# A gated linear attention followed by a SoLU layer: two kinds of small matmul cut into pieces of 32 weight columns

## The chip, the core and the metric

The kernel runs on one core of a Trainium2 chip, in one launch. The metric is device time in microseconds, the median of several executions. One further execution was profiled; every duration, wait and order in time below is from that one. TensorE appears in the profile as two rows, PE for matmuls and PEld for weight loads; VectorE is DVE, ScalarE is ACT, GpSimd is POOL, SyncE is SP.

## What is computed

Four batch entries, eight heads, 768 steps, head dimension 48. A complex state is decayed and updated at each step; the output is read from its real part. Its result, 3072 tokens of 384, goes through a two-layer network of width 1024 with a softmax gate and a layer norm between:

```python
mag = np.sqrt(a_re * a_re + a_im * a_im)
scale = np.minimum(mag, 0.999) / (mag + 1e-06)
for t in range(S):
    new_re = ar * S_re - ai * S_im
    new_im = ar * S_im + ai * S_re
    S_re, S_im = (new_re + einsum('bhd,bhe->bhde', k[t], v[t]), new_im)
    y[:, :, t] = einsum('bhd,bhde->bhe', q[t], S_re)
x = y.transpose(0, 2, 1, 3).reshape(B * S, H * D)
h = x @ w_in
solu = h * softmax(h)
ln = (solu - mean) / np.sqrt(var + 1e-06) * g_ln
out = ln @ w_out
```

All data is fp32.

## The kernel before

The recurrence is computed in chunks of 128 steps, six chunks in time (`ti`) for each of four batch entries (`b`), so 24 chunks in all. The complex decay is turned into cumulated magnitudes and phases, and q and k are multiplied by them with cosine and sine side by side (`f_q2`, `f_k2`: 96 columns a head). Within a chunk the steps are then plain matmuls. The main loop is unrolled: each turn weaves together the preparation of the next `ti` (`prep_steps`), the attention of chunk n (`chunk_steps`), the network of chunk n-1 (`ffn_steps`), and the turning of q and k of chunk n+1 (`turn_steps`). There is a second, general program (`general`) in the file; a flag computed at run time decides whether it is needed, and it is not run here.

The steps that the change and the prediction touch:

- `score` (L768): for each head, scores of a chunk, keys by queries, 128 x 128 over a contraction of 96, into `f_score`. VectorE masks them into `f_att` (L770), half a chunk (four heads) at a time.
- `values` (L774 to L786): for each head, `f_att` (128 x 128) is the stationary operand (`lhsT`, "weights") and the head's 48 columns of v stream through (L779). From the second `ti` on a second matmul adds the contribution of the state: the queries `f_qT` (96 x 128) are the weights, and 48 columns of `f_state` stream (L782). Both write the same 128 partitions x 48 columns of one PSUM bank, the tile `f_y`. VectorE copies the tile to `f_xn` (L785).
- `carry` (L788 to L800): for each head, `f_k2` (128 x 96) is the weights and the 48 columns of v stream, into 96 partitions of the tile `f_d`, which has the same single PSUM buffer as `f_y` (pool `f_ps_y`). VectorE adds it to the state and GpSimd multiplies it by the chunk's total decay.
- `ffn_steps`: `f_xt` is the transposed x (L814), `f_h` = x by `w_in` (two halves of three products of 512 columns, L824), the maximum (L832), the exponential (L833), the product `f_z` (L836), its transposes `f_zt` (L845), the statistics, and `f_o` = z by `w_out` (eight products of 384 columns, L870).
- `f_turned` (L747) are the transposes of q and k; `f_L` (L659) and `f_phase` (L700, L703) are the cumulated sums of `prep_steps`; `f_tot` (L684) is a transpose of 32 rows, five times in all; `f_count` (L889) is a one-column matmul at the end of the attention, once.

The order on TensorE, VectorE, GpSimd and SyncE is set by the framework's scheduler, which takes the instructions in the woven order and places them by its own costs and by what is ready; only ScalarE's order is that of the program. Each queue is then in order. SyncE issues all DMAs. An fp32 product becomes two weight loads and two matmuls in the trace (384 matmuls at L779 for 24 x 8 products); the transposes become one of each.

Of the kernel before, what the change touches and what calls it, by code (L numbers as in the profile page):

```python
# [17 lines left out]
P = 128  # L18
# [493 lines left out]
def whole(ctx, tc, flag, q, k, v, a_re, a_im, moe_w_in, moe_w_out, moe_g_ln, out):  # L512
# [8 lines left out]
    nc = tc.nc  # L521
    B, H, S, D = q.shape
    D2 = 2 * D
# [28 lines left out]
    state = [const.tile([D2, DM], FP, name=f"f_state{b}") for b in range(B)]  # L552

    seen = const.tile([P, 3, NC], FP, name="f_seen")
    T = {}

    def heads(t):
        return t.rearrange("p (h d) -> p h d", d=D)
# [198 lines left out]
    def chunk_steps(ti, b):  # L757
        st = {}

        def score(half):  # L760
            def f():
                if half == 0:
                    st["att"] = two.tile([P, H, P], FP, tag="att", name="f_att")
                QT, KT = T["qT", ti, b], T["kT", ti, b]
                ps = ps_s.tile([P, 4, P], FP, tag="s", name="f_score")
                for i in range(4):
                    x = half * 4 + i
                    nc.tensor.matmul(out=ps[:, i], lhsT=KT[:, x * P:(x + 1) * P], rhs=QT[:, x * P:(x + 1) * P],  # L768
                                     start=True, stop=True)
                nc.vector.tensor_tensor(out=st["att"][:, half * 4:half * 4 + 4], in0=ps,  # L770
                                        in1=tri.unsqueeze(1).to_broadcast([P, 4, P]), op=OP.mult)
            return f

        def values():  # L774
            V = T["v", ti][:, b]
            y = ps_y.tile([P, DM], FP, tag="y", padded_shape=[P, 512], name="f_y")
            for x in range(H):
                ys = y[:, x * D:(x + 1) * D]
                nc.tensor.matmul(out=ys, lhsT=st["att"][:, x], rhs=V[:, x * D:(x + 1) * D], start=True,  # L779
                                 stop=(ti == 0))  # L780
                if ti > 0:
                    nc.tensor.matmul(out=ys, lhsT=T["qT", ti, b][:, x * P:(x + 1) * P],  # L782
                                     rhs=state[b][:, x * D:(x + 1) * D], start=False, stop=True)
            xt = xp.tile([P, DM], FP, tag="x", name="f_xn")
            nc.vector.tensor_copy(out=xt, in_=y)  # L785
            T["x", ti, b] = xt  # L786

        def carry():  # L788
            V = T["v", ti][:, b]
            d = ps_y.tile([D2, DM], FP, tag="y", padded_shape=[P, 512], name="f_d")  # L790
            for x in range(H):
                nc.tensor.matmul(out=d[:, x * D:(x + 1) * D],  # L792
                                 lhsT=T["k2", ti, b][:, x].rearrange("p u d -> p (u d)"),
                                 rhs=V[:, x * D:(x + 1) * D], start=True, stop=True)
            tot = T["tot", ti][:, b * H:(b + 1) * H].unsqueeze(2).to_broadcast([D2, H, D])
            if ti > 0:
                nc.vector.tensor_tensor(out=state[b], in0=d, in1=state[b], op=OP.add)  # L797
                nc.gpsimd.tensor_tensor(out=heads(state[b]), in0=heads(state[b]), in1=tot, op=OP.mult)  # L798
            else:
                nc.vector.tensor_tensor(out=heads(state[b]), in0=heads(d), in1=tot, op=OP.mult)  # L800

        steps = [score(0), score(1), values]
        if ti < NC - 1:
            steps.append(carry)
        return steps
# [106 lines left out]
    for n in range(len(chunks) + 1):  # L912
        ti, b = chunks[n] if n < len(chunks) else (NC, 0)
# [76 lines left out]
```

## Time and profile before

| | |
|---|---|
| median of 3 runs | 747.02 us (746.8 to 751.04) |
| the profiled execution | 743.38 us |
| its span, first to last instruction | 741.6 us |
| mean granted TensorE clock over the span | 0.878 |
| PE busy / PEld busy | 588.8 us / 416.1 us, 2887 instructions each |
| VectorE, ScalarE, GpSimd busy | 380.3, 246.4, 171.3 us |
| f_y, value part (L779) | 384 matmuls, mean 285 ns |
| f_y, state part (L782) | 320 matmuls, mean 290 ns |
| f_d (L792) | 320 matmuls, mean 286 ns |

A row of the profile names the line, the engine, the operation, the tile written and the tiles read, the shape and the count, then busy time, the mean of one in ns, and the idle time of the engine just before with what ended it. In a row of the timeline the first number is the start and the second the length of a merged group. Matmuls are pipelined: the mean of one contains the latency of reading its operands, several are in flight, and the distance between starts is less than the duration. In the views by stretches of time each engine has its busy time and its count, then come the granted clock, the share of the DMA engines and the bandwidth.

### The profile page before, as it was taken

The page shows a single profiled execution, that of the slowest core. Times are in us where ns is not written, and L with a number is a line of the kernel's source. Part 1 is how long each engine was busy: PE and PEld are TensorE (multiplying, and loading weights), DVE is VectorE, ACT ScalarE, POOL GpSimd, SP SyncE. Part 2 cuts the span into 40 slices and gives each one's busy share as a digit, 9 for nine tenths or more (in the row PEclk, how much of TensorE's full clock was granted, in tenths as well). Part 3 has the DMA queues.
Part 4 walks back from the last instruction along what each step waited for, and adds up shares of the span by engine and source line. Part 5 has one row for each costly group of instructions (what it writes and reads, how often), then busy time and mean ns, then how long its engine had stood idle before and what let it go on. Part 6 is the DMA issues. An engine that isn't in the chain of part 4 may idle for free. (4 is left out here: it accounts for less than half of the span.)

```text
span 741.6 us, 7378 instructions
## 1 busy us (share of the span) xinstructions
PE 588.8 (79%) x2887; PEld 416.1 (56%) x2887; DVE 380.3 (51%) x590; ACT 246.4 (33%) x325; POOL 171.3 (23%) x133
## 2 busy tenths in 40 slices
PE   0215217768998988998988989898989989999994
PEld 0104204535667665767665766675766757766652
DVE  2489985646526447525537344457354673322331
ACT  2435040214234354236233244334343542222211
POOL 2072565530112050221222021412020420000000
PEclk9955658669996999998989999989989999999997
DMA  9834722040420050520040420223310000000000
GB/s 170 159 74 100 132 64 64 22 82 15 96 54 0 11 97 0 96 54 6 6 96 7 89 54 11 56 42 69 62 20 11 12 0 11 11 11 11 11 11 17
DMA packets 131788, 35.55 MB, mean 48 GB/s; under 512 B 126752, under 2 KB 129824, under 8 KB 131744
## 3 DMA queue, kind: packets, MB, share of 16 engines
q1 hardware_dynamic: 131744, 34.98, 23.9%
q8 instruction: 25, 0.41, 0.2%
q14 instruction: 19, 0.16, 0.1%
HBM read 30.22 MB, written 4.72 MB: 47 GB/s over the span
## 5 line engine op out<-in xcount | busy, mean ns | idle before, releaser
L870 PE MATMUL f_o<-f_w_out,f_zT 128*128 128x384 f32 x384 | 139.8, 512 | 0.0
L824 PE MATMUL f_h<-f_w_in,f_xT 128*128 128x512 f32 x288 | 130.8, 597 | 0.6 <-ACT f_xT L817 0.6
L870 PEld LDWEIGHTS f_o<-f_w_out,f_zT 128*128 128x128 f32 x384 | 74.4, 204 | 44.0 <-issue 7.0
L862 POOL TENSOR_TENSOR f_s<-f_s,f_mv 128x1 f32<-128x1 f32 x24 | 19.7, 822 | 314.5 <-DVE f_s L861 186.0
L824 PEld LDWEIGHTS f_h<-f_w_in,f_xT 128*128 128x128 f32 x288 | 53.2, 190 | 58.8 <-issue 51.7
L779 PE MATMUL f_y<-f_v,f_att 128*128 128x48 f32 x384 | 73.2, 285 | 14.6 <-DVE f_att L770 14.5
L833 ACT ACTIVATE f_z<-f_h,f_nmax 128x1024 f32<-128x1024 f32 x24 | 26.7, 1113 | 148.0 <-DVE f_nmax L832 125.3
L779 PEld LDWEIGHTS f_y<-f_v,f_att 128*128 128x128 f32 x384 | 61.1, 204 | 19.7 <-DVE f_att L770 15.4
L782 PE MATMUL f_y<-f_state,f_qT 96*128 96x48 f32 x320 | 65.9, 290 | 0.0
L832 DVE TENSOR_REDUCE f_nmax<-f_h 128x1 f32<-128x1024 f32 x24 | 29.3, 1223 | 60.0 <-PE f_h L824 60.0
L768 PEld LDWEIGHTS f_score<-f_qT,f_kT 96*128 96x128 f32 x384 | 53.2, 201 | 9.3 <-issue 6.8
L768 PE MATMUL f_score<-f_qT,f_kT 96*128 96x128 f32 x384 | 56.9, 283 | 0.0
L876 DVE TENSOR_SCALAR f_ot<-f_o,f_rs 128x384 f32<-128x384 f32 x24 | 14.8, 616 | 77.4 <-PE f_o L870 38.5
L750 ACT COPY f_kT<-f_turned 96x512 f32<-96x512 f32 x48 | 27.8, 579 | 80.2 <-PE f_turned L747 80.2
L792 PE MATMUL f_d<-f_v,f_k 128*96 128x48 f32 x320 | 40.0, 286 | 16.7 <-DVE f_xn L785 16.7
L782 PEld LDWEIGHTS f_y<-f_state,f_qT 96*128 96x128 f32 x320 | 52.7, 206 | 0.0
L792 PEld LDWEIGHTS f_d<-f_v,f_k 128*96 128x96 f32 x320 | 39.3, 207 | 19.5 <-DVE f_xn L785 17.6
L770 DVE TENSOR_TENSOR f_att<-f_score,f_mats 128x512 f32<-128x512 f32 x48 | 32.9, 685 | 28.5 <-PE f_score L768 28.5
L659 PE MATMUL f_L<-f_lr,f_mats 128*128 128x384 f32 x48 | 21.3, 538 | 32.6 <-DVE f_lr L652 32.6
L846 ACT COPY f_zT<-f_zt 128x512 f32<-128x512 f32 x48 | 26.5, 585 | 59.6 <-PE f_zt L845 59.6
L750 ACT COPY f_qT<-f_turned 96x512 f32<-96x512 f32 x48 | 28.0, 583 | 52.9 <-PE f_turned L747 52.8
L798 POOL TENSOR_TENSOR f_state<-f_state,f_tot 96x384 f32<-96x384 f32 x16 | 19.1, 1192 | 112.3 <-DVE f_state L797 110.7
(93 smaller groups left out, 896.1 us busy)
## 6 DMA issues: line engine op xcount, KB each, us to landing
f_ar<-in_a_re_dram SPq DMA_DIRECT2D x24, 192.0 KB, 4.0
f_ai<-in_a_im_dram SPq DMA_DIRECT2D x24, 192.0 KB, 4.5
f_q<-in_q_dram SPq DMA_DIRECT2D x24, 192.0 KB, 4.5
f_k<-in_k_dram SPq DMA_DIRECT2D x24, 192.0 KB, 4.0
f_v<-in_v_dram SPq DMA_DIRECT2D x24, 192.0 KB, 4.2
out_dram<-f_ot SPq DMA_DIRECT2D x24, 192.0 KB, 2.0
f_raw<-in_moe_w_in_dram SPq DMA_DIRECT2D x6, 512.0 KB, 4.6
f_raw<-in_moe_w_out_dram SPq DMA_DIRECT2D x8, 384.0 KB, 3.1
```

The costliest lines, as they stand in the source:

```text
L659: nc.tensor.matmul(out=ps, lhsT=tri, rhs=lm, start=True, stop=True)
L750: nc.scalar.copy(out=T[nm + "T", ti, b][:, half * 512:half * 512 + 512], in_=ps[0:D2].rearrange("p i t -> p (i t)"))
L768: nc.tensor.matmul(out=ps[:, i], lhsT=KT[:, x * P:(x + 1) * P], rhs=QT[:, x * P:(x + 1) * P], start=True, stop=True)
L770: nc.vector.tensor_tensor(out=st["att"][:, half * 4:half * 4 + 4], in0=ps, in1=tri.unsqueeze(1).to_broadcast([P, 4, P]), op=OP.mult)
L779: nc.tensor.matmul(out=ys, lhsT=st["att"][:, x], rhs=V[:, x * D:(x + 1) * D], start=True, stop=(ti == 0))
L782: nc.tensor.matmul(out=ys, lhsT=T["qT", ti, b][:, x * P:(x + 1) * P], rhs=state[b][:, x * D:(x + 1) * D], start=False, stop=True)
L792: nc.tensor.matmul(out=d[:, x * D:(x + 1) * D], lhsT=T["k2", ti, b][:, x].rearrange("p u d -> p (u d)"), rhs=V[:, x * D:(x + 1) * D], star ...
L824: nc.tensor.matmul(out=st["h"][:, half * 512:(half + 1) * 512], lhsT=st["xT"][:, c * P:(c + 1) * P], rhs=w_in[:, c, half * 512:(half + 1) ...
L832: nc.vector.tensor_reduce(out=nmax, in_=st["h"], op=OP.max, axis=AX.X, negate=True)
L833: nc.scalar.activation(out=st["z"], in_=st["h"], func=AF.Exp, bias=nmax, accum_out=st["se"])
L846: nc.scalar.copy(out=st["zT"][:, half * 512:(half + 1) * 512], in_=ps)
L870: nc.tensor.matmul(out=st["o"], lhsT=st["zT"][:, c * P:(c + 1) * P], rhs=w_out[:, c], start=(c == 0), stop=(c == KF - 1))
```

## The change

The two matmuls of `values` and the one of `carry` are written as loops over groups of 32 weight columns. Each piece takes 32 columns of the weights, streams the same 48 columns through them, and writes the group of 32 PSUM partitions that belongs to those columns. `values` has four groups, `carry` three. The order within a head is: the four value pieces, then the four state pieces. Operands, buffers, results and all other steps are as before.

```diff
--- before.py
+++ after.py
@@ -774,13 +774,15 @@
         def values():
             V = T["v", ti][:, b]
             y = ps_y.tile([P, DM], FP, tag="y", padded_shape=[P, 512], name="f_y")
+
             for x in range(H):
-                ys = y[:, x * D:(x + 1) * D]
-                nc.tensor.matmul(out=ys, lhsT=st["att"][:, x], rhs=V[:, x * D:(x + 1) * D], start=True,
-                                 stop=(ti == 0))
-                if ti > 0:
-                    nc.tensor.matmul(out=ys, lhsT=T["qT", ti, b][:, x * P:(x + 1) * P],
-                                     rhs=state[b][:, x * D:(x + 1) * D], start=False, stop=True)
+                hs = slice(x * D, (x + 1) * D)
+                for g in range(0, P, 32):
+                    nc.tensor.matmul(out=y[g:g + 32, hs], lhsT=st["att"][:, x, g:g + 32], rhs=V[:, hs], start=True,
+                                     stop=(ti == 0))
+                for g in range(0, P if ti > 0 else 0, 32):
+                    nc.tensor.matmul(out=y[g:g + 32, hs], lhsT=T["qT", ti, b][:, x * P + g:x * P + g + 32],
+                                     rhs=state[b][:, hs], start=False, stop=True)
             xt = xp.tile([P, DM], FP, tag="x", name="f_xn")
             nc.vector.tensor_copy(out=xt, in_=y)
             T["x", ti, b] = xt
@@ -789,9 +791,9 @@
             V = T["v", ti][:, b]
             d = ps_y.tile([D2, DM], FP, tag="y", padded_shape=[P, 512], name="f_d")
             for x in range(H):
-                nc.tensor.matmul(out=d[:, x * D:(x + 1) * D],
-                                 lhsT=T["k2", ti, b][:, x].rearrange("p u d -> p (u d)"),
-                                 rhs=V[:, x * D:(x + 1) * D], start=True, stop=True)
+                hs, k2 = slice(x * D, (x + 1) * D), T["k2", ti, b][:, x].rearrange("p u d -> p (u d)")
+                for g in range(0, D2, 32):
+                    nc.tensor.matmul(out=d[g:g + 32, hs], lhsT=k2[:, g:g + 32], rhs=V[:, hs], start=True, stop=True)
             tot = T["tot", ti][:, b * H:(b + 1) * H].unsqueeze(2).to_broadcast([D2, H, D])
             if ti > 0:
                 nc.vector.tensor_tensor(out=state[b], in0=d, in1=state[b], op=OP.add)
```

On TensorE 352 products of f_y become 1408 and 160 of f_d become 480. The framework gives each piece an array shape of 128 rows by 32 columns, where the whole products have 128 by 128. Of the other matmuls of the program that runs only `f_tot` (32 by 128) and `f_count` (128 by 32) have a shape of their own. Between neighbours on TensorE the shape changes 120 times after the change and 12 times before. The scheduler also orders anew; line numbers behind the change have moved (L779 is L781, L782 is L784, L792 is L796, L845 is L847, L870 is L872).

The first place is on TensorE in a later chunk, of the second batch entry, at the end of `values` (the number at the end of a name is a buffer's). Before:

```order
L779 MATMUL f_y<-f_v,f_att 128x48
L782 MATMUL f_y<-f_state_119,f_qT 128x48
L845 MATMUL f_zt<-f_mats,f_z 128x128 x8
L792 MATMUL f_d<-f_v,f_k_900 96x48 x3
L870 MATMUL f_o<-f_w_out,f_zT 128x384 x8
L684 MATMUL f_tot<-f_mats,f_e_1252 96x32
L747 MATMUL f_turned<-f_mats,f_k_918 96x128 x4
L792 MATMUL f_d<-f_v,f_k_900 96x48 x5
```

With the change:

```order
L781 MATMUL f_y<-f_v,f_att 32x48 x4
L784 MATMUL f_y<-f_state_119,f_qT 32x48 x3
L847 MATMUL f_zt<-f_mats,f_z 128x128 x8
L784 MATMUL f_y<-f_state_119,f_qT 32x48
L781 MATMUL f_y<-f_v,f_att 32x48 x4
L784 MATMUL f_y<-f_state_119,f_qT 32x48 x4
L872 MATMUL f_o<-f_w_out,f_zT 128x384 x7
L684 MATMUL f_tot<-f_mats,f_e_1524 96x32
L747 MATMUL f_turned<-f_mats,f_k_1038 96x128 x4
L747 MATMUL f_turned<-f_mats,f_q_1029 96x128 x4
L872 MATMUL f_o<-f_w_out,f_zT 128x384
L796 MATMUL f_d<-f_v,f_k_1020 32x48 x24
```

The eight transposes f_zt now stand inside f_y, with nine of its 64 pieces behind them, and f_d, which stood in two parts around f_o, now stands in one part behind it.

The second place is on TensorE in a chunk of the first `ti`, where there is no state part yet. Before:

```order
L779 MATMUL f_y<-f_v,f_att 128x48 x8
L792 MATMUL f_d<-f_v,f_k_262 96x48 x8
L845 MATMUL f_zt<-f_mats,f_z 128x128 x8
L747 MATMUL f_turned<-f_mats,f_k_888 96x128 x4
L870 MATMUL f_o<-f_w_out,f_zT 128x384 x4
```

With the change:

```order
L781 MATMUL f_y<-f_v,f_att 32x48 x32
L847 MATMUL f_zt<-f_mats,f_z 128x128 x8
L796 MATMUL f_d<-f_v,f_k_262 32x48 x4
L747 MATMUL f_turned<-f_mats,f_k_1008 96x128 x4
L872 MATMUL f_o<-f_w_out,f_zT 128x384 x4
L747 MATMUL f_turned<-f_mats,f_q_995 96x128 x4
L872 MATMUL f_o<-f_w_out,f_zT 128x384 x4
L796 MATMUL f_d<-f_v,f_k_262 32x48 x20
```

Here f_d stood directly behind f_y and now comes behind f_zt, in two parts with transposes and f_o between them.

## The prediction

> **What bounds the kernel now.** I read the page's busy shares and slices first, then the same by stretches of time, then who waits for whom.
>
> ```profile
> PE 588.8 (79%) x2887; PEld 416.1 (56%) x2887; DVE 380.3 (51%) x590; ACT 246.4 (33%) x325; POOL 171.3 (23%) x133
> PE   0215217768998988998988989898989989999994
> PEclk9955658669996999998989999989989999999997
> 320.00:426.00 106.00, 96.40 (x503) 70.25 (x502) 53.26 (x82) 40.61 (x54) 22.82 (x17) 0.94 0.22 45
> 426.00:532.00 106.00, 96.39 (x503) 70.17 (x502) 53.42 (x83) 40.63 (x54) 22.82 (x17) 0.94 0.23 45
> L832 DVE TENSOR_REDUCE f_nmax<-f_h 128x1 f32<-128x1024 f32 x24 | 29.3, 1223 | 60.0 <-PE f_h L824 60.0
> ```
>
> From about 200 us on TensorE is the bound: in each 106 us (four chunks, one for each batch index) PE is busy 96.4, VectorE 53, and VectorE's longest idle time ends with a matmul. The granted clock there is 0.94, so work that is costed at full clock is stretched by about 1/0.93 = 1.075 (0.92 to 0.94 in the five stretches from 215 us on). What a product costs on PE therefore goes almost whole into the time. The next question is what paces the products that are split.
>
> ```profile
> L779 PE MATMUL f_y<-f_v,f_att 128*128 128x48 f32 x384 | 73.2, 285 | 14.6 <-DVE f_att L770 14.5
> L782 PE MATMUL f_y<-f_state,f_qT 96*128 96x48 f32 x320 | 65.9, 290 | 0.0
> L792 PE MATMUL f_d<-f_v,f_k 128*96 128x48 f32 x320 | 40.0, 286 | 16.7 <-DVE f_xn L785 16.7
> 415.97 0.39 PE L782 MATMUL f_y<-f_state,f_qT 96*128 96x48 f32 x2
> ...
> 419.10 0.39 PE L782 MATMUL f_y<-f_state,f_qT 96*128 96x48 f32 x2
> 419.32 1.06 PE L845 MATMUL f_zt<-f_mats,f_z 128*128 128x128 f32 x8
> 421.15 2.75 PE L870 MATMUL f_o<-f_w_out,f_zT 128*128 128x384 f32 x8
> 423.73 0.60 PE L747 MATMUL f_turned<-f_mats,f_q 128*96 128x128 f32 x4
> 426.75 0.97 PE L792 MATMUL f_d<-f_v,f_k 128*96 128x48 f32 x10
> 427.56 0.61 PE L747 MATMUL f_turned<-f_mats,f_k 128*96 128x128 f32 x4
> L779 PEld LDWEIGHTS f_y<-f_v,f_att x384: 186/192/338, 74.0 to 707.3; 128*128 128x128 f32 x192
> L792 PEld LDWEIGHTS f_d<-f_v,f_k x320: 159/165/284, 87.9 to 635.5; 128*96 128x96 f32 x160
> ```
>
> Twenty-four chunks of 8 heads are 192 products at L779, and the trace has 384: an fp32 product runs as two passes, each with its own weight load. Durations of matmuls overlap, so I take distances between starts. From 415.97 to 419.10 lie 14 rows of two passes: 3.13/28 = 112 ns a pass. f_o streams 384 columns in (423.73 - 421.15)/8 = 322 ns, 0.84 ns a column; at that rate a pass over 48 columns needs 40 ns, so f_y is not paced by its matmul. The load of 96 weight columns (median 165 ns) is 27 ns shorter than that of 128 (192), again 0.84 ns a column, and f_d's passes come every (427.56 - 426.75)/10 = 81 ns. Both are paced by weight columns: 128 x 0.84 = 108 and 4 over for f_y, 96 x 0.84 = 81 for f_d. At full clock f_y costs 352 products x 2 x 112 = 78.8 us and f_d 160 x 2 x 81 = 25.9: 104.7 us, a seventh of the span.
>
> **The change, part by part.**
>
> *The passes.* 352 products of f_y become 1408 pieces, 160 of f_d become 480. That is 1888 pieces, 3776 passes for 1024. Weight columns in total are the same, bytes streamed as moving operand are three to four times as many. A pass now has 32 x 0.84 = 27 ns of load and 40 ns of streaming. If different column groups stream at the same time, while loads still come one after another with the 4 ns that f_y's pass has beyond its columns, a pass costs 31 ns. The bounds of this unknown are wide. Below: the two passes of one piece use the same group and cannot share it, so a piece takes at least one 40 ns stream plus 4, with its other pass beside the neighbour's first: 44 ns a piece, 22 a pass. Above: 81 ns, the fastest sustained pass that the trace shows, as if a pass could not be issued faster. I take 31, because loads that stand one behind another are what paces these very rows now. f_y: 8 x 31 - 224 = +24 ns a product, 352 of them, +8.4 us. f_d: 6 x 31 - 162 = +24 ns, 160 of them, +3.8. Together +12.2.
>
> *Going in and out of the narrow form.* All but six matmuls of the path that runs use the array in one shape. One exception is the count of L889, one column wide, and it shows what an excursion costs.
>
> ```profile
> 677.02 0.59 ACT L750 COPY f_qT<-f_turned 96x512 f32<-96x512 f32 x1
> 677.56 0.39 PE L768 MATMUL f_score<-f_qT,f_kT 96*128 96x128 f32 x2
> 677.88 0.09 PEld L889 LDWEIGHTS f_count<-f_good,f_mats 128*1 128x1 f32 x2
> 677.88 0.20 PE L889 MATMUL f_count<-f_good,f_mats 128*1 128x18 f32 x2
> 678.01 0.71 PE L768 MATMUL f_score<-f_qT,f_kT 96*128 96x128 f32 x4
> 678.12 0.17 DVE L892 TENSOR_REDUCE f_total<-f_count 1x1 f32<-1x18 f32 x1 [1.34 <-PE f_count L889]
> 678.56 0.59 PE L824 MATMUL f_h<-f_w_in,f_xT 128*128 128x512 f32 x1
> L889 PE MATMUL f_count<-f_good,f_mats x2: 178/178/178, 677.9 to 677.9; 128*1 128x18 f32 x2
> ```
>
> From 677.56 to 678.56 run six score passes and two of the count. Six at 112 are 0.67 us; two matmuls of 178 ns fill 0.20, so they start about 25 ns apart, 0.05 for both. The other 0.28 us is neither: the count's input was ready (VectorE had been idle 1.34 us) and the buffer's last reader, at 677.02, had ended by 677.61. So 0.28 us is what one trip out of the full shape and back costs. The Trainium skill, TensorEngine Tiling, Key Properties, says that a change of tiling mode drains the engine; the trace agrees with 0.28 us, and without that rule the same row would be called a chance gap and this term nothing. In the changed order 120 neighbours differ in shape where 12 did: 54 more trips, 54 x 0.28 = 15.1 us. Below, nothing, if a long matmul ahead hides the drain; above, this sum. I take the sum, since nothing in that row hid it.
>
> *What is moved.* The scheduler now cuts f_y around f_zt and moves f_d behind f_o. The cut is in the trips. The copy f_xn comes some 0.9 us later there, behind eight transposes, but seven f_o passes cover it before f_d needs the bank. No DMA and no VectorE, ScalarE or GpSimd instruction is added.
>
> *What swallows part.* PE itself waits in places:
>
> ```profile
> PE f_y L779 <- DVE f_att L770: 14.5, 5, 3.6
> PE f_zt L845 <- DVE f_se L860: 12.7, 6, 3.9
> 417.62 1.23 DVE L836 TENSOR_TENSOR f_z<-f_h,f_z 128x1024 f32<-128x1024 f32 x1 [0.67 <-ACT f_z L833]
> ```
>
> Growth ahead of such a wait costs nothing: 8 products x 24 ns x 5 and 16 x 24 ns x 6, about 3 us.
>
> *The sum*, at full clock 12.2 + 15.1 = 27.3, times 1.075 = 29, less 3: +26 us. The profiled execution took 743.38 us (span 741.6), so 769; the runs' median of 747.02 lies 3.6 above it, so I forecast 773 on the runs' scale. Its own range is 757 to 782 (trips free; trips as said and 33 ns a pass).
>
> **The rivals.**
>
> *Groups work fully side by side.* Loads of different groups overlap too, and a piece costs the lower bound of 44 ns: f_y 4 x 44 - 224 = -48 ns, -16.9 us; f_d 3 x 44 - 162 = -30, -4.8. With the trips that is -21.7 + 15.1 = -6.6, times 1.075 -7: 736, on the runs' scale 740; with trips hidden -23 (724). The place is the f_y stretch, and the deciding price is a piece of (104.7 - 15.1)/1888 = 47 ns: under it the change is not slower. For it: the pieces write different partitions. The Trainium skill, TensorEngine Tiling, Key Properties, says that different tiles can load and multiply in parallel; no row here shows it. Against it: part cannot be collected. f_z is done at 418.85 and f_zt starts at 419.32, so f_y may end at most 0.47 us sooner in such a chunk, where 16 products would save 0.77; with half of the twenty later chunks so, 3 us are lost.
>
> *Streams take turns.* Matmuls of different groups do not overlap; each pass costs 40 + 4 = 44 ns. f_y 8 x 44 - 224 = +128, +45.1 us; f_d 6 x 44 - 162 = +102, +16.3. With trips 76.5, times 1.075 82, less up to 4 in waits: +78, 821, on the runs' scale 825. For it: every stream in the trace is one after another. Against: none there uses another group.
>
> *Instructions can't be had fast enough.* The passes bring 5504 more instructions to PE's queue.
>
> ```profile
> 725.90 0.72 PEld L845 LDWEIGHTS f_zt<-f_mats,f_z 128*128 128x128 f32 x4 [4.70 <-issue]
> 725.93 0.88 PE L845 MATMUL f_zt<-f_mats,f_z 128*128 128x128 f32 x3 [3.90 <-DVE f_se L860]
> ```
>
> After a wait, with PE empty, the matmul starts 30 ns behind its load. At 30 ns an instruction, 60 a pass, f_y grows by 256 ns (90.1 us), f_d by 198 (31.7); with trips 137, times 1.075 147: 890, and 894 on the runs' scale. At 81 a pass it would be 979. Against it: the count's two passes start 25 ns apart, though four waiting instructions say little on a stream of 256. The Trainium skill, TensorE: Matmul & The Clock Gate, Part 1, gives about 62 ns a matmul where the sequencer decodes in its own code; by that figure my estimate is 902 on the runs' scale; no row here tells which way it is decoded.
>
> **How the numbers follow.** The forecast has 0.45, side by side 0.22, taking turns 0.20, instructions 0.13. The range 734 to 833 holds the forecast, taking turns, and side by side with its trips; left out are the instructions and part of side by side with trips hidden, under 2 in 10. About 1% is what a measurement of this kernel can tell from no change. Faster by over 1% needs side by side with trips largely hidden, half of its chance: 0.11. Within 1%: its other half and the forecast's low end, 0.11 + 0.06 = 0.17. Slower: 0.72.
>
> **What would show it.** In the profile after: f_y's passes start about 31 ns apart (rows of four pieces, eight passes, every 250 ns), and the first full-width row after a stretch comes some 0.2 us late. Distances of 22 ns would show side by side, 44 turns, 60 or more the supply of instructions. Granted clock in the stretches stays between 0.90 and 0.95. The forecast is wrong if f_y's stretch of 16 products, 3.5 us before, gets shorter, or takes more than 5 us; or if f_y keeps to 4 us and the time still moves by over 5%.

## The result: 4.3% faster

| | before | after |
|---|---|---|
| median | 746.91 us (4 runs) | 716.14 us (4 runs) |
| ratio, 95% interval | | 0.957 (0.951 to 0.963) |
| span of the profiled execution | 741.6 us | 714.8 us |
| PE busy / the rest of the span | 588.8 / 152.8 us | 533.9 / 180.9 us |

The forecast was 773, slower, with a range down to 734. The time lies outside it and on the other side. The page of the changed kernel, first the busy shares, the granted clock by slices, and the groups that answer to those shown of before:

```profile
PE 533.9 (75%) x5639; PEld 344.4 (48%) x5639; DVE 379.4 (53%) x590; ACT 245.7 (34%) x325; POOL 170.6 (24%) x133
PEclk9955658769997989997989997999989999999998
L781 PE MATMUL f_y<-f_v,f_att 128*32 128x48 f32 x1536 | 39.6, 214 | 21.8 <-DVE f_att L770 21.8
L847 PE MATMUL f_zt<-f_mats,f_z 128*128 128x128 f32 x192 | 31.9, 320 | 25.0 <-DVE f_se L862 16.5
L796 PE MATMUL f_d<-f_v,f_k 128*32 128x48 f32 x960 | 24.7, 240 | 21.2 <-DVE f_xn L787 21.2
```

PE's busy time fell by 54.9 us though it has nearly twice the instructions; its idle time rose by 28.1; the difference, 26.8, is what the span lost. Three waits hold most of the rise: for f_att 21.8 us (14.5 before), ahead of f_zt 25.0 (12.7), for f_xn 21.2 (16.7), together 24. (f_se, named ahead of f_zt, is an operation of 0.14 us right behind f_z on VectorE; what f_zt reads is f_z.) So there are two things to explain: why the pieces are so much cheaper than forecast, and where half of that went. The timeline of one chunk of the changed kernel answers both:

```profile
402.05 0.29 PE L781 MATMUL f_y<-f_v,f_att 128*32 128x48 f32 x8
402.16 0.27 PE L784 MATMUL f_y<-f_state,f_qT 96*32 96x48 f32 x8
...
402.69 0.27 PE L784 MATMUL f_y<-f_state,f_qT 96*32 96x48 f32 x8
403.14 0.29 PE L781 MATMUL f_y<-f_v,f_att 128*32 128x48 f32 x8 [0.19 <-DVE f_att L770]
...
403.78 0.27 PE L784 MATMUL f_y<-f_state,f_qT 96*32 96x48 f32 x8
405.13 1.06 PE L847 MATMUL f_zt<-f_mats,f_z 128*128 128x128 f32 x8 [1.09 <-DVE f_z L838]
412.66 0.79 PE L796 MATMUL f_d<-f_v,f_k 128*32 128x48 f32 x40
413.38 0.64 PE L747 MATMUL f_turned<-f_mats,f_k 128*96 128x128 f32 x4
```

From 402.16 to 402.69 six rows of eight passes start, one product each: 88 ns a product, 11 ns a pass, where a product took 224 before. That is two streams of 40 ns plus 4 for eight passes, so all four column groups stream at once, and the loads of their weights (32 columns, 27 ns at 0.84 a column) overlap too: four loads fit into 44 ns. f_d's 40 passes take 0.72 us with the way out of the narrow shape (some 0.14), 14 to 15 a pass at full clock: three groups at once, 86 ns a product for 162. And PE now stands still: at the seam between the halves of `f_att`, and for 1.09 us ahead of f_zt, where before f_z had been ready 0.47 us early.

### The profile page after: what moved, and what is told of

Read it like the earlier page. It is cut to its first block, busy times and chain, and to the rows that moved or that the text cites. A ratio compares the mean times of both kernels' runs of the same rounds, so it can differ in the third digit from the quotient of the medians.

```text
span 714.8 us, 12886 instructions
## 1 busy us (share of the span) xinstructions
PE 533.9 (75%) x5639; PEld 344.4 (48%) x5639; DVE 379.4 (53%) x590; ACT 245.7 (34%) x325; POOL 170.6 (24%) x133
## 5 line engine op out<-in xcount | busy, mean ns | idle before, releaser
L872 PE MATMUL f_o<-f_w_out,f_zT 128*128 128x384 f32 x384 | 143.2, 520 | 0.3 <-ACT f_zT L848 0.3
L872 PEld LDWEIGHTS f_o<-f_w_out,f_zT 128*128 128x128 f32 x384 | 75.3, 207 | 44.2 <-issue 8.0
L781 PE MATMUL f_y<-f_v,f_att 128*32 128x48 f32 x1536 | 39.6, 214 | 21.8 <-DVE f_att L770 21.8
L768 PEld LDWEIGHTS f_score<-f_qT,f_kT 96*128 96x128 f32 x384 | 50.8, 193 | 9.3 <-issue 6.8
L768 PE MATMUL f_score<-f_qT,f_kT 96*128 96x128 f32 x384 | 54.8, 277 | 0.0
L847 PE MATMUL f_zt<-f_mats,f_z 128*128 128x128 f32 x192 | 31.9, 320 | 25.0 <-DVE f_se L862 16.5
L781 PEld LDWEIGHTS f_y<-f_v,f_att 128*32 128x32 f32 x1536 | 32.1, 113 | 30.4 <-DVE f_att L770 24.2
L747 PE MATMUL f_turned<-f_mats,f_k 128*96 128x128 f32 x192 | 37.1, 326 | 13.0 <-DVE f_k L724 8.4
L796 PE MATMUL f_d<-f_v,f_k 128*32 128x48 f32 x960 | 24.7, 240 | 21.2 <-DVE f_xn L787 21.2
L847 PEld LDWEIGHTS f_zt<-f_mats,f_z 128*128 128x128 f32 x192 | 25.4, 164 | 28.7 <-issue 15.8
```

Source lines behind the costliest of these rows:

```text
L747: nc.tensor.transpose(out=ps[0:D2, i], in_=T[nm + "2", ti, b][:, half * 4 + i].rearrange("p u d -> p (u d)"), identity=ident)
L781: nc.tensor.matmul(out=y[g:g + 32, hs], lhsT=st["att"][:, x, g:g + 32], rhs=V[:, hs], start=True, stop=(ti == 0))
L796: nc.tensor.matmul(out=d[g:g + 32, hs], lhsT=k2[:, g:g + 32], rhs=V[:, hs], start=True, stop=True)
L847: nc.tensor.transpose(out=ps[:, i * P:(i + 1) * P], in_=st["z"][:, c * P:(c + 1) * P], identity=ident)
L872: nc.tensor.matmul(out=st["o"], lhsT=st["zT"][:, c * P:(c + 1) * P], rhs=w_out[:, c], start=(c == 0), stop=(c == KF - 1))
```

## The experiments

The theory: column groups have queues and streams of their own, so a product costs two streams; what TensorE saves is partly waited away for VectorE. The rivals: narrow pieces are cheap whatever group they use; the gain comes from the new order of the other instructions; the trips between shapes are free. Ratios are to the kernel before on the same chip, with 95% intervals.

**The same pieces, one group behind the other.**

```diff
-            for x in range(H):
-                hs = slice(x * D, (x + 1) * D)
-                for g in range(0, P, 32):
+            for x0, g in ((x0, g) for x0 in range(0, H, 4) for g in range(0, P, 32)):
+                for x in range(x0, x0 + 4):
+                    hs = slice(x * D, (x + 1) * D)
                     nc.tensor.matmul(out=y[g:g + 32, hs], lhsT=st["att"][:, x, g:g + 32], rhs=V[:, hs], start=True,
                                      stop=(ti == 0))
-                for g in range(0, P if ti > 0 else 0, 32):
-                    nc.tensor.matmul(out=y[g:g + 32, hs], lhsT=T["qT", ti, b][:, x * P + g:x * P + g + 32],
-                                     rhs=state[b][:, hs], start=False, stop=True)
+                    if ti > 0:
+                        nc.tensor.matmul(out=y[g:g + 32, hs], lhsT=T["qT", ti, b][:, x * P + g:x * P + g + 32],
+                                         rhs=state[b][:, hs], start=False, stop=True)
```

> The same pieces as in the change, as many trips between shapes, but ordered so that the pieces of one column group stand behind one another (four heads of one group, then four of the next). Theory A, groups stream side by side and a group can't overlap with itself: a pass costs the 40 ns stream plus 4 again, a product of f_y 8 x 44 = 352 ns for 87 now, 352 products, +93 us at full clock, about +100 by the granted clock, of which up to 20 vanish in waits: 795 to 816 us. Rival B, narrow pieces are quick in themselves, whatever group they use: starts stay 6 to 11 ns apart and the time stays at 716 within 1%. Rival C, the gain came from the new order of the other instructions, which this kernel shares: 716 too, but with starts 44 ns apart.

735.68 us, ratio 0.986 (0.980 to 0.992): 20 us more than the change, not 80. Its timeline:

```profile
401.83 0.27 PE L781 MATMUL f_y<-f_v,f_att 128*32 128x48 f32 x2
401.94 0.25 PE L784 MATMUL f_y<-f_state,f_qT 96*32 96x48 f32 x2
402.03 0.25 PE L781 MATMUL f_y<-f_v,f_att 128*32 128x48 f32 x2
402.12 0.25 PE L784 MATMUL f_y<-f_state,f_qT 96*32 96x48 f32 x2
402.20 0.25 PE L781 MATMUL f_y<-f_v,f_att 128*32 128x48 f32 x2
402.29 0.25 PE L784 MATMUL f_y<-f_state,f_qT 96*32 96x48 f32 x2
402.38 0.28 PE L781 MATMUL f_y<-f_v,f_att 128*32 128x48 f32 x4
402.46 0.28 PE L784 MATMUL f_y<-f_state,f_qT 96*32 96x48 f32 x4
402.58 0.25 PE L781 MATMUL f_y<-f_v,f_att 128*32 128x48 f32 x2
...
402.93 0.28 PE L781 MATMUL f_y<-f_v,f_att 128*32 128x48 f32 x4
```

Within one group two passes start every 87 to 90 ns, 44 a pass: a group can't overlap with itself, and the passes cost four times as much as when the next one uses another group. That ends the rival of cheap narrow pieces. The order of the other instructions is the change's, and the time is 736 and not 716, so that order alone does not bring the gain. But at the seams (rows of four) the last passes of one group run beside the first of the next, so 16 passes take 0.55 us (402.38 to 402.93), not 0.70: a product costs 275 ns, not 352, and f_y 66 us more than in the change. Why only 20 of these come out, the waits and the windows of this kernel tell:

```profile
PE f_d L796 <- DVE f_xn L787: 15.4, 7, 11.2
PE f_y L781 <- DVE f_att L770: 12.4, 5, 2.8
PE f_zt L847 <- DVE f_se L862: 10.4, 6, 3.9
PE f_zt L847 <- DVE f_z L838: 0.9, 1, 0.9
```

```profile
207.00:308.00 101.00, 91.21 (x956) 63.42 (x955) 54.02 (x80) 38.99 (x52) 20.50 (x16) 1.00 0.25 45
308.00:408.00 100.00, 91.60 (x991) 65.00 (x991) 52.97 (x79) 39.05 (x52) 22.70 (x15) 0.97 0.26 48
```

The waits for f_att, f_z (with f_se) and f_xn are 39 us where the change has 68, and the granted clock is 0.97 to 1.00 in these stretches, where the change has:

```profile
207.00:308.00 101.00, 85.93 (x1009) 56.96 (x1008) 53.52 (x82) 40.20 (x54) 21.98 (x16) 0.92 0.26 48
308.00:408.00 100.00, 84.93 (x1004) 56.14 (x1004) 53.40 (x82) 40.27 (x54) 23.00 (x17) 0.91 0.26 49
```

Slower matmuls fill the waits, and the clock comes back. The first is a matter of counting; what moves the clock was not tried. It is no small term. Against the kernel before, this one pays 18 us more for f_y (275 ns for 224) and up to 14 for the trips, and saves 12 at f_d: some 20 us more at full clock, and yet it takes 10 us less. PE's idle time is nearly the same, 148.5 us for 152.8; the mean granted clock over the span is 0.927 for 0.878, worth some 32 us on 581 us of matmuls (an estimate). The change itself has 0.885, so by the same estimate the clock makes no more than some 4 us of its gain.

**Four passes of one group in a row.**

```diff
                 for g in range(0, P, 32):
                     nc.tensor.matmul(out=y[g:g + 32, hs], lhsT=st["att"][:, x, g:g + 32], rhs=V[:, hs], start=True,
                                      stop=(ti == 0))
-                for g in range(0, P if ti > 0 else 0, 32):
-                    nc.tensor.matmul(out=y[g:g + 32, hs], lhsT=T["qT", ti, b][:, x * P + g:x * P + g + 32],
-                                     rhs=state[b][:, hs], start=False, stop=True)
+                    if ti > 0:
+                        nc.tensor.matmul(out=y[g:g + 32, hs], lhsT=T["qT", ti, b][:, x * P + g:x * P + g + 32],
+                                         rhs=state[b][:, hs], start=False, stop=True)
```

> The change with each group's value piece and state piece of a head behind one another: four passes of one group in a row, then the next group. If passes must start in program order, as the forecast had it, they go three serial passes of 44 ns and then one beside the next group's first: a head costs 4 x 132 + 44 = 572 ns for 174, 160 heads, +64 us at full clock, and some 20 in the time as with 16 in a row (736). If each group has a short queue of its own, four passes deep or more by what the seams of the run with 16 in a row show: a head still costs 174 to 200 ns and the time is 716 within 1%.

716.04 us, ratio 0.959 (0.952 to 0.966): the same as the change. The program, in the order that the scheduler leaves on TensorE, alternates value and state, a piece (two passes) at a time; the starts do not:

```profile
403.94 0.31 PE L781 MATMUL f_y<-f_v,f_att 128*32 128x48 f32 x8
404.05 0.29 PE L784 MATMUL f_y<-f_state,f_qT 96*32 96x48 f32 x8
404.14 0.29 PE L781 MATMUL f_y<-f_v,f_att 128*32 128x48 f32 x7
404.23 0.21 PE L784 MATMUL f_y<-f_state,f_qT 96*32 96x48 f32 x1
404.24 0.21 PE L781 MATMUL f_y<-f_v,f_att 128*32 128x48 f32 x1
```

Eight value passes, of all four groups, start ahead of the first state pass, though the program has two, then two of the other, and so on. So passes of different groups start out of program order; four in a row are held back for their group while the others go on, and 16 in a row are too many, where only the seams overlap. The Trainium skill, TensorE: Matmul & The Clock Gate, Part 3 (The mechanism), says that matmuls start and end in program order; these rows show that matmuls of different column groups do not start in it, and the measurement decides. So the sentence ahead of the prediction that each queue is in order does not hold for these matmuls.

**Half of the change, and the other half.** Values in pieces with the state update whole, and the reverse. The first undoes this part of the change, the second the part in `values`:

```diff
-                for g in range(0, D2, 32):
-                    nc.tensor.matmul(out=d[g:g + 32, hs], lhsT=k2[:, g:g + 32], rhs=V[:, hs], start=True, stop=True)
+                nc.tensor.matmul(out=d[:, x * D:(x + 1) * D],
+                                 lhsT=T["k2", ti, b][:, x].rearrange("p u d -> p (u d)"),
+                                 rhs=V[:, x * D:(x + 1) * D], start=True, stop=True)
```

> Only the matmuls of values in pieces, the state update whole. At full clock f_y saves (224 - 87) ns x 352 = 48 us of TensorE's time; 35 more trips between shapes, some 0.16 us each by the trace of the change, take 6. If everything TensorE saves came out: 747 - 45 = 702. If, as in the whole change, about half comes out and the rest turns into waits: 722 to 728. If the state update carries most of the gain: 740 or more.

> Only the state update in pieces, values whole. f_d saves about (162 - 66) ns x 160 = 15 us; 32 more trips of 0.16 us take 5. All out: 736. Half out: 741 to 743. If the parts add, this and the run with values alone together give the change's 31 us; if a wait is shared between them, together they give more than 31.

727.64 us, ratio 0.974 (0.969 to 0.980), and 738.22 us, ratio 0.989 (0.983 to 0.995). The first has its half coming out as expected. For the second the expectation counted too much: with 86 ns a product f_d saves 12 us and not 15, and with the 0.26 us a trip that is measured below 32 trips take 8, which leaves 4 at full clock. The measured 8 us (4 to 12 by the interval) are all of that or more, not half; in its profiled execution PE's busy time is 8.1 us less than before and the span 5.4. Within the intervals of about 0.6% each the parts add: 2.6% and 1.1% against 4.3% in the whole.

**Pieces of 64 columns**, in values alone; the state update is whole, as before.

```diff
-                for g in range(0, P, 32):
-                    nc.tensor.matmul(out=y[g:g + 32, hs], lhsT=st["att"][:, x, g:g + 32], rhs=V[:, hs], start=True,
+                for g in range(0, P, 64):
+                    nc.tensor.matmul(out=y[g:g + 64, hs], lhsT=st["att"][:, x, g:g + 64], rhs=V[:, hs], start=True,
                                      stop=(ti == 0))
-                for g in range(0, P if ti > 0 else 0, 32):
-                    nc.tensor.matmul(out=y[g:g + 32, hs], lhsT=T["qT", ti, b][:, x * P + g:x * P + g + 32],
+                for g in range(0, P if ti > 0 else 0, 64):
+                    nc.tensor.matmul(out=y[g:g + 64, hs], lhsT=T["qT", ti, b][:, x * P + g:x * P + g + 64],
                                      rhs=state[b][:, hs], start=False, stop=True)
```

> Values in two pieces of 64 columns instead of four of 32, the state update whole; to be compared with the run that splits values alone into 32. Theory A with loads of different groups side by side: a pass is paced by its own load of 64 columns, 54 + 4 = 58 ns, two groups at once, a product 2 x 58 = 116 ns for 87: 10 us more at full clock, 3 to 10 us in the time. Rival, loads stand one behind another: 4 x 58 = 232 ns a product, no faster than whole, 745 or more.

733.93 us, ratio 0.982 (0.975 to 0.989), 6 us more than the run with 32 columns.

```profile
392.19 0.22 PE L781 MATMUL f_y<-f_v,f_att 128*64 128x48 f32 x1
392.20 0.27 PE L784 MATMUL f_y<-f_state,f_qT 96*64 96x48 f32 x2
...
392.66 0.22 PE L781 MATMUL f_y<-f_v,f_att 128*64 128x48 f32 x1
```

Between the first and the last of these rows 16 passes start, 0.47 us, 29 ns a pass and 117 ns a product, against 116 expected. A pass is paced by its own load of 64 columns, and loads of two groups run at once: the load is divided among the groups, and at 32 weight columns the 48 streamed ones pace it.

**What a trip costs.** Value part in pieces, state part whole, so that the shape changes twice in each head.

```diff
-                for g in range(0, P if ti > 0 else 0, 32):
-                    nc.tensor.matmul(out=y[g:g + 32, hs], lhsT=T["qT", ti, b][:, x * P + g:x * P + g + 32],
+                if ti > 0:
+                    nc.tensor.matmul(out=y[:, hs], lhsT=T["qT", ti, b][:, x * P:(x + 1) * P],
                                      rhs=state[b][:, hs], start=False, stop=True)
```

> Values in pieces, the state part of f_y whole, head by head: the shape changes 406 times instead of 120, 143 more trips, and 160 products cost 224 ns again for 87 (22 us at full clock). A trip at 0.28 us, as forecast: 22 + 40, times 1.075 67, less up to 20 in waits: 763 to 783. A trip at 0.16 us, as the change's trace has it (0.09 late on the way in, 0.06 on the way out): 22 + 23, times 1.075 48, less up to 20: 744 to 764. No cost of a trip: 720 to 740.

773.54 us, ratio 1.030 (1.018 to 1.041); one of the four runs took 762.7.

```profile
395.25 0.29 PE L781 MATMUL f_y<-f_v,f_att 128*32 128x48 f32 x8
395.47 0.42 PE L784 MATMUL f_y<-f_state,f_qT 96*128 96x48 f32 x2
395.82 0.29 PE L781 MATMUL f_y<-f_v,f_att 128*32 128x48 f32 x8
396.04 0.42 PE L784 MATMUL f_y<-f_state,f_qT 96*128 96x48 f32 x2
396.39 0.29 PE L781 MATMUL f_y<-f_v,f_att 128*32 128x48 f32 x8
```

A head takes (396.39 - 395.25)/2 = 0.57 us, where its parts need 0.09 and 0.22: a trip out and back costs 0.26 us, 0.13 on each way (0.22 less 0.09 from a value row to a state row, 0.35 less 0.22 back). My 0.16, read from the change's trace, was too low on both. The 0.28 of the forecast, from a single one-column matmul, was near, and the rule of the Trainium skill, TensorEngine Tiling (Array Packing), Key Properties, that a change of mode drains the engine, agrees with it. The price rests on these rows and not on the total: from 207 to 608 us the granted clock of this run is 0.85 to 0.88, where the change has 0.91 to 0.95.

**Where the other half went.** The product f_z in two halves, so that the first four transposes need only the first; once with pieces, once with whole products.

```diff
-            nc.vector.tensor_tensor(out=st["z"], in0=st["h"], in1=st["z"], op=OP.mult)
+            for i in range(0, FF, 512):
+                z = st["z"][:, i:i + 512]
+                nc.vector.tensor_tensor(out=z, in0=st["h"][:, i:i + 512], in1=z, op=OP.mult)
```

> The change, with the product f_z on VectorE in two halves of 512, so that the first four transposes f_zt can start a half (0.6 us) sooner. In the change's trace f_zt waits 25 us for VectorE, in 23 places. Theory: that wait now takes back part of the gain; 23 x 0.6 = 14 us at most, 5 to 12 less in the time, 704 to 711. Rival, the waits are not what holds it (what is won at f_zt is waited for at the next place): 716 within 4.

> The kernel before with the same halves of f_z and whole products. There f_zt waits 12.7 us in 6 places, and f_z is ready 0.47 us before f_zt starts in a chunk of the middle. Theory: at most 6 x 0.6 = 4 us less, 743 or unchanged. If halves of f_z help here as much as with the pieces, the wait has nothing to do with the change.

With pieces 703.65 us, ratio 0.943 (0.938 to 0.948), 12.5 us less than the change. With whole products 750.11 us, ratio 1.003 (1.000 to 1.007): nothing. The same edit is worth 12 us or nothing, depending on whether f_y leaves time for f_z. The waits of the first:

```profile
PE f_y L781 <- DVE f_att L770: 21.1, 16, 4.5
PE f_zt L849 <- DVE f_z L840: 12.9, 19, 3.3
```

The wait ahead of f_zt is halved, from 25.0, with 3.6 us more ahead of f_o; the one for f_att is as it was. (The profiled execution took 708.96 us, the longest of its five.) This is the fastest kernel of the study.

**Two attempts at more.** The maximum over f_h in halves as well (the first taken while the second half of f_h is multiplied, the two joined by a minimum of the negated values); and, in another kernel, the copy f_xn on ScalarE. Both start from the run with f_z in halves. The first, then the second:

```diff
                     nc.tensor.matmul(out=st["h"][:, half * 512:(half + 1) * 512], lhsT=st["xT"][:, c * P:(c + 1) * P],
                                      rhs=w_in[:, c, half * 512:(half + 1) * 512], start=(c == 0), stop=(c == KD - 1))
+                st["m", half] = sml.tile([P, 1], FP, tag=f"m{half}", name="f_m")
+                nc.vector.tensor_reduce(out=st["m", half], in_=st["h"][:, half * 512:(half + 1) * 512], op=OP.max,
+                                        axis=AX.X, negate=True)
...
-            nc.vector.tensor_reduce(out=nmax, in_=st["h"], op=OP.max, axis=AX.X, negate=True)
+            nc.vector.tensor_tensor(out=nmax, in0=st["m", 0], in1=st["m", 1], op=OP.min)
```

```diff
-            nc.vector.tensor_copy(out=xt, in_=y)
+            nc.scalar.copy(out=xt, in_=y)
```

> The run with f_z in halves, and the maximum over f_h in halves too, the first one taken while the second half of f_h is multiplied. The chain behind f_h gets about 0.5 us shorter once more; the scheduler also puts f_d ahead of f_zt in most chunks, which fills the wait there with 1 us of matmuls. Theory: another 5 to 10 us less than with f_z in halves alone, 697 to 706. If TensorE's own work is the bound again by then: no less than f_z in halves alone.

> The run with f_z in halves (703.7), with the copy f_xn moved from VectorE (0.56 us a chunk) to ScalarE, which is busy 40 of 100 us. Theory: VectorE's queue is what the matmuls wait for now (f_att, f_z), so 0.56 us less on it in each chunk brings 3 to 8 us: 696 to 701. Rival: ScalarE's order is fixed, the copy waits there for f_y and holds up the exponential or the copies behind it: 704 or more.

726.57 us, ratio 0.974 (0.969 to 0.979), and 728.13 us, ratio 0.975 (0.968 to 0.982): both lose more than 20 us to the run with f_z in halves alone. The waits of the first, then of the second:

```profile
PE f_d L796 <- DVE f_xn L787: 36.3, 11, 12.1
PE f_zt L852 <- DVE f_z L843: 28.2, 20, 3.8
PE f_y L781 <- DVE f_att L770: 1.8, 3, 1.1
```

```profile
PE f_zt L849 <- DVE f_z L840: 28.0, 20, 4.2
PE f_d L796 <- ACT f_xn L787: 24.3, 2, 20.5
```

In the first the scheduler did put f_d ahead of f_zt, where it waits for the copy f_xn: 36.3 us for 21.3 with f_z in halves alone. The wait ahead of f_zt rose as well, 28.2 for 12.9, and the one for f_att went, 1.8 for 21.1; the three together are 11 us more, of 21 by which PE's idle time rose (188.4 for 167.1). In the second f_zt waits 28.0 for 12.9. The waits of f_d for the copy came to 24.3 for 21.3, nearly all in one of 20.5. Both theories failed; the second run fits its rival in the time (704 or more), but that the copy holds up the exponential is not shown. Which orders on VectorE and ScalarE bring this about was not taken further.

## Why the prediction was wrong, step by step

- *What bounds the kernel* was right: PE. "Goes almost whole into the time" holds in one direction. PE gave back 55 us and the time 27. In the quoted chunks 0.47 us of slack ahead of f_zt became a wait of 1.09.
- *The pace of the passes before* (112 and 81 ns, set by weight columns) was right.
- *The passes after* is the step that failed. I took 31 ns, bounds 22 and 81; measured at full clock are 11 for f_y and 14 to 15 for f_d. Both the value and its lower bound rested on sentences about order: that loads stand one behind another, and that "the two passes of one piece use the same group and cannot share it, so a piece takes at least one 40 ns stream plus 4, with its other pass beside the neighbour's first". The first half of that is true (44 ns a pass in one group). The second assumed that a matmul that waits for its group holds up the next one. It does not. The lower bound should have been the busiest group's own streams, two a product: 88 ns, 11 a pass. With it the term is (88 - 224) x 352 + (86 - 162) x 160 ns = -60 us, not +12.
- *The trips* were near in price (0.28 forecast, 0.26 in the run that alternates), so at most 54 x 0.26 = 14 us. How many of them end in a wait, as the one ahead of f_zt does, and cost less was not counted.
- *The sum* with these two terms is -46 us at full clock, -50 by the factor of 1.075. PE's idle time took 28 of that back, which leaves -22 for a measured -27 in the span; the other 5 are not assigned (a mean granted clock of 0.885 for 0.878 is worth some 4 on 534 us, an estimate). The waits are the second term that failed: I had put them at 3 us, counting only what growth they swallow, and 3 more for f_z under the rival, where the runs show 28.
- *The rival* of groups side by side was the right mechanism. I gave it 0.22 and 740 or 724; its price carried the same wrong lower bound, and the measured 716 lies under both. Its break-even of 47 ns for a piece was met with 22 (29 for f_d). The sentence of the Trainium skill, TensorEngine Tiling (Array Packing), Key Properties, that different tiles load and multiply in parallel, for which no row stood then, is borne out by 11 ns a pass. The rivals of turns and of instruction supply are out: eight passes, 16 instructions, start every 88 ns.
- *What would show it*: its first sign of being wrong came, "f_y's stretch of 16 products, 3.5 us before, gets shorter". It is 1.8 us with the wait inside.

## What to carry to other kernels

A product that is paced by loading its weights (many weight columns, few streamed ones) gets faster when it is cut by weight columns into groups that write different partitions: loads and streams of the groups overlap, and the price is the busiest group's own streams, plus about a quarter of a microsecond for each stretch in the narrow shape. Bound such a cost below by what one resource must do, not by an order that no row has shown. And before counting a gain, look at how much slack the next wait has: here an edit to VectorE's work that was worth nothing became worth 12 us as soon as the matmuls ahead of it got short.

## What was not expected of the hardware

- Matmuls of different column groups start out of program order; four passes in a row to one group cost nothing, sixteen do (275 ns a product for 88).
- Loads of different column groups overlap: four of 32 columns (27 ns each at 0.84 a column) in 44 ns, two of 64 columns (54 ns) in 58.
- The granted clock was 0.97 to 1.00 in the middle stretches of the kernel with one group behind the other, 0.91 to 0.92 in the same stretches of the change, and 0.85 to 0.88 in those of the run that changes shape in every head. Its cause stays open.
